# Linear attention with a gated feed-forward network: write-back of weight halves and sums as one transfer each, under another order of all steps

## The chip, the cores and the metric

One Trainium2 chip; the kernel runs on one of its cores. The metric is the time of one execution on the device, in microseconds. The time of a kernel is the median of its runs.

## The reference

The inputs are q, k, v of shape [8, 8, 576, 64] (batch, heads, sequence, head dimension), three weight matrices and a gain. All arrays are float32, but the weights reach the device as 64-bit words and are turned into float32 there. Cut to what matters:

```
q_s = softmax(q, over the head dimension)        # + 1e-9 in the denominator
k_s = softmax(k, over the sequence)              # + 1e-9 in the denominator
kv  = einsum('bhsd,bhse->bhde', k_s, v)
x   = einsum('bhsd,bhde->bhse', q_s, kv)  ->  [4608, 512]   # tokens x (8 heads x 64)
xn  = x / sqrt(mean(x*x) + 1e-6) * rms_g
g   = xn @ w_gate                                # 512 -> 1536
out = (g * sigmoid(g) * (xn @ w_val)) @ w_out    # 1536 -> 512
```

## The kernel before

**Tiling.** The 4,608 tokens are cut into 9 blocks of 512 (TB). The 1,536 columns of the hidden layer are cut into 12 slices of 128 (NF); a step that works on slice i of block j is numbered s = 12 j + i. The eight heads are handled as four pairs (the second index g of the attention steps). So that TensorE can use its faster 32-bit format and still come near float32, an operand is split in two: a rounded upper half ("hi") and the rest ("lo"), and a product is made of hi x hi, hi x lo and lo x hi.

**Attention of a block.** For each pair of heads: k_load and v_load, then k_max (in block 0 k_max0, L522, three instructions), k_tr (L531, a transpose on TensorE), k_top (L537), k_diag (L541, the identity scaled by the column maxima: one instruction, on VectorE unless another engine is named), k_rows (L545, a matmul that spreads the maxima over all rows; the tiles of both lie in ps_a, in ps_o for block 0), k_sub, k_exp, k_mm (L560, the product with v, which has a column of ones from v_ones for the sum), k_eps and k_rec. The kv matrix goes to kv_hi and kv_lo, or for block 0 to kv_norm0 (L611, two instructions), into tiles that kv_zero has cleared on GpSimd. The query side is q_load (L627, 8 or 16 transfers; in blocks 0 and 1 q_load0, L639, fewer; three buffers "qt"), maximum, q_sub, q_exp, sum, q_eps, q_rec, q_mul (in blocks 0 and 1 the steps with a 0 at the end), a transpose, a copy out of PSUM (q_c0, L685, in blocks 0 and 1), and the product with kv (q_x). From that come x_hi (L777) and x_lo, the squares x_sq (L782), and the norm: n_sum0 (L813) in block 0, n_sum in the others, and n_y, n_rows.

**Weights.** load_w brings 512 KB of a slice (gate, value or output part) as words into one of the buffers of RAW (L376 to L378). These repeat: load_w.4 uses the buffer of slice 0 and load_w.5 that of slice 1, so each waits for the conversion of its predecessor (conv_mul, conv_shift, conv_sign, conv_low, conv_add). w_hi (L878) and w_lo (L881) split the gate and value parts, o_hi and o_lo the output part.

**Blocks 0 to 2** are done directly: f1 (L950) makes 12 matmuls for the gate and 12 for the value, g_mul, silu and h_mul combine them, h_hi and h_lo split the result, f2 (L984) makes 12 matmuls (8 where the slice is not split) that add up in four PSUM tiles, and store scales and writes them.

**Blocks 3 to 8** are done as three pairs of blocks. For each pair the first layer is a product of 2 x 2 quarters by Strassen's scheme: step pp (L1101) makes one of seven products k, whose left side is a quarter of the weights (A11, A12, A21, A22) or a sum of quarters (S1 to S4), and whose right side is a block part or a sum of parts (t_add, split by b_hi and b_lo). The c_ steps (L1122 among them) combine products, gate and hm form the hidden values, hp_hi and hp_lo split them, f2p (L1188) makes the 12 matmuls of the second layer, and put (L1191) copies one PSUM tile of 128 tokens into a buffer "ot" (two of them; for the last block's tiles 2 and 3 a buffer "gs") and writes it out; the very last tile, put.2.1.3, is split between ScalarE and VectorE.

**Scratch in memory.** During block 1 (s = 12 to 23) the split weights are written back to scratch tensors in device memory, on SP's queue: w_keep (L897) the gate and value part of a slice, o_keep (L903) the output part, s_keep (L944) one of the four sums of a pair of slices. Each does this as two transfers: w_keep and s_keep one for the gate (m = 0) and one for the value (m = 1), o_keep one for hi and one for lo. The scratch of the gate and that of the value are tensors of their own, wd[i][0] and wd[i][1], for each of six pairs of slices i. In block 2, w_back (L907, slices 30 to 35) and o_back (L914) read them again on GpSimd's queue, and in the pairs w_in (L1068) reads quarters and sums and o_in (L1076) the output parts.

**The order.** The text ORDER (L22 on) lists 3,101 steps. The loop at L1216 to L1221 runs through it; a letter behind a step names the engine for its copy, scaling or elementwise instruction (A ScalarE, D VectorE, P GpSimd), through copy (L386), scaled (L390) and on (L383). Each engine executes its own instructions in the order of the text, and so do the queues that issue transfers: SP all loads and all writes, GpSimd w_back, o_back, w_in and o_in. warm.n (L453) puts n matmuls with no use into the first microseconds.

Of the kernel before, what the change touches and what calls it, by code (L numbers as in the profile page):

```python
# [22 lines left out]
constants exp_table k_load.0.0 q_load0.0.0 v_ones.0.0 warm.9 q_load0.0.2 kv_zero0.0 v_ones.0.2 v_ones.0.3 v_ones.0.1  # L23
q_load0.0.1 kv_zero0.1 kv_zero.4 k_load.0.2 kv_zero.5 v_load.0.0 kv_zero.6 kv_zero.7 kv_zero.0 k_load.0.3 kv_zero.1
q_load0.0.3 kv_zero.2 k_max0.0.0 kv_zero.3 k_load.0.1 q_max0.0.0 v_load.0.2 k_tr.0.0 warm.2.0 k_top.0.0 q_sub0.0.0:P
q_max0.0.2 v_load.0.3 k_diag.0.0:A k_rows.0.0 q_max0.0.1 warm.2.1 q_sub0.0.2:P g_load q_exp.0.0 k_sub.0.0 v_load.0.1
q_sub0.0.1:P q_exp.0.2 q_sum0.0.0 load_w.0.0 k_exp.0.0 load_w.0.1 q_sum0.0.2 load_w.1.0 q_exp.0.1 k_max0.0.2 k_mm.0.0
load_w.1.1 k_load.1.0 q_eps0.0.0 q_eps0.0.2 k_tr.0.2 warm.2.2 q_rec0.0.0 k_max0.0.3 warm.2.10 load_w.0.2 q_rec0.0.2
q_mul0.0.0:P k_tr.0.3 k_top.0.2 load_w.2.0 q_max0.0.3 k_diag.0.2:A load_w.2.1 k_rows.0.2 q_mul0.0.2:P q_sum0.0.1
q_t0.0.0 q_load0.1.0 k_top.0.3 k_sub.0.2 q_sub0.0.3:P k_diag.0.3:A warm.2.11 q_c0.0.0:A k_rows.0.3 warm.2.3 k_eps.0.0  # L30
k_exp.0.2 load_w.1.2 k_sub.0.3 q_t0.0.2 load_w.3.0 q_exp.0.3 load_w.3.1 k_max0.0.1 k_mm.0.2 k_exp.0.3 load_w.2.2
load_w.3.2 q_eps0.0.1 k_rec.0.0 q_c0.0.2:A q_rec0.0.1 k_load.1.1 k_tr.0.1 q_sum0.0.3 warm.2.13 q_mul0.0.1:P
kv_norm0.0.0:A k_mm.0.3 k_top.0.1 k_eps.0.2 k_diag.0.1:A q_eps0.0.3 k_rec.0.2 conv_mul.0.0 q_load0.1.1 q_rec0.0.3
k_rows.0.1 k_eps.0.3 q_mul0.0.3:P q_x0.0.0 k_sub.0.1 kv_norm0.0.2:A conv_low.0.0.1 q_t0.0.1 k_rec.0.3 conv_shift.0.0
k_exp.0.1 q_load0.1.2 conv_sign.0.0 q_x0.0.2 x_hi.0.0:A conv_add.0.0.1 q_c0.0.1:A x_lo.0.0 warm.2.12 x_sq.0.2 warm.2.5
x_sq.0.0 k_mm.0.1 x_hi.0.2:A q_t0.0.3 conv_mul.0.1 k_eps.0.1 x_lo.0.2 kv_norm0.0.3:A v_ones.1.0 conv_shift.0.1 n_sum0.0
v_load.1.0 q_c0.0.3:A k_rec.0.1 conv_sign.0.1 conv_low.0.1.1 warm.2.6 q_x0.0.3 k_max.1.0 kv_norm0.0.1:A conv_add.0.1.1
conv_mul.1.0 q_x0.0.1 x_sq.0.3 conv_shift.1.0 w_hi.0.0.2:A warm.2.4 x_hi.0.1:D warm.2.8 conv_sign.1.0 x_sq.0.1 warm.2.7
w_lo.0.0:P x_hi.0.3:A f1.0.0.0.0 x_lo.0.1 n_sum0.1 conv_mul.1.1 x_lo.0.3 w_lo.0.1:P f1.0.0.0.1 conv_low.1.0.2 n_sum0.2
conv_shift.1.1 q_max0.1.0 f1.0.0.0.2 conv_low.0.2.1 n_sum0.3 conv_sign.1.1 q_sub0.1.0:P conv_low.2.0.2 f1.0.0.0.3 n_t.0  # L40
f1.0.1.0.0 f1.0.0.1.0 conv_add.1.0.2 f1.0.1.0.1 conv_mul.0.2 n_y0.0 f1.0.1.0.2 f1.0.1.0.3 f1.0.0.1.1 q_exp.1.0
conv_shift.0.2 f1.0.0.1.2 f1.0.0.1.3 conv_low.1.2.1 f1.0.1.1.0 n_y1.0 f1.0.1.1.1 f1.0.1.1.2 f1.0.1.1.3 f1.0.0.2.0
w_hi.1.0.2:A f1.0.0.2.1 f1.0.0.2.2 f1.0.0.2.3 f1.0.1.2.0 conv_low.3.0.2 conv_sign.0.2 w_lo.1.0:P f1.0.1.2.1 f1.0.1.2.2
f1.0.1.2.3 n_rows.0 k_tr.1.0 conv_low.2.2.1 conv_add.0.2.1 k_top.1.0 g_mul.0 k_diag.1.0:A k_rows.1.0 q_sum0.1.0 f1.1.0
silu.0 w_lo.1.1:P load_w.4.0 k_sub.1.0 load_w.4.1 load_w.4.2 n_cols.0 v_ones.1.1 v_load.1.1 conv_mul.2.0 q_eps0.1.0
h_mul.0 conv_mul.2.1 conv_shift.2.0 f1.1.1 k_exp.1.0 conv_shift.2.1 conv_sign.2.0 conv_sign.2.1 conv_mul.1.2 q_rec0.1.0
f2.0 conv_add.2.0.2 g_mul.1 conv_mul.3.0 conv_shift.1.2 conv_low.3.2.1 conv_shift.3.0 silu.1 conv_sign.1.2 q_mul0.1.0:P
conv_sign.3.0 w_hi.2.0.2:A h_mul.1 conv_add.1.2.1 k_mm.1.0 q_load0.1.3 k_max.1.1 conv_mul.3.1 warm.2.9 w_lo.2.0:P
f1.2.0 conv_low.4.0.2 k_eps.1.0 load_w.5.0 conv_shift.3.1 load_w.5.1 w_lo.2.1:P conv_low.4.2.1 k_rec.1.0 load_w.5.2
conv_sign.3.1 k_load.1.2 kv_norm0.1.0:A q_max0.1.1 conv_add.3.0.2 conv_mul.2.2 q_t0.1.0 g_mul.2 kv_hi.1.0:A f1.2.1  # L50
q_c0.1.0:A conv_shift.2.2 silu.2 q_max0.1.2 conv_mul.4.0 conv_sign.2.2 q_sub0.1.1:P w_hi.3.0.2:A conv_shift.4.0
conv_add.2.2.1 q_x0.1.0 q_max0.1.3 q_exp.1.1 conv_sign.4.0 f2.1 w_lo.3.1:P load_w.6.0 x_hi.1.0:D load_w.6.1 x_sq.1.0
# [5 lines left out]
load_w.8.2 w_lo.4.1:P conv_sign.5.1 conv_mul.5.2 q_sum0.1.2 conv_add.5.0.2 k_tr.1.1 f1.4.0 o_hi.4:A k_top.1.1 h_mul.3
k_diag.1.1:A conv_shift.5.2 q_sum0.1.3 conv_low.7.0.2 o_lo.4:P conv_sign.5.2 k_rows.1.1 f1.4.1 k_sub.1.1 w_hi.5.0.2:A
conv_add.5.2.1 g_mul.4 k_exp.1.1 q_eps0.1.1 w_lo.5.0:P load_w.10.0 q_rec0.1.1 load_w.10.1 f2.3 load_w.10.2 q_mul0.1.1:D  # L60
conv_mul.6.0 w_lo.5.1:P conv_mul.6.1 q_load.2.0 conv_shift.6.0 silu.4 conv_shift.6.1 conv_sign.6.0 conv_sign.6.1
k_mm.1.1 o_hi.5:A h_mul.4 conv_add.6.0.2 conv_mul.7.0 f1.5.0 k_eps.1.1 h_hi.4:A k_rec.1.1 k_load.1.3 conv_shift.7.0
kv_norm0.1.1:A conv_sign.7.0 conv_low.8.0.2 h_lo.4:P q_t0.1.1 g_mul.5 w_hi.6.0.2:A f1.5.1 q_c0.1.1:D o_lo.5:P
conv_mul.7.1 conv_mul.6.2 conv_shift.7.1 w_lo.6.0:P silu.5 conv_shift.6.2 conv_low.7.2.1 conv_sign.7.1 w_lo.6.1:P f2.4
conv_low.8.2.1 conv_sign.6.2 conv_mul.7.2 conv_add.7.0.2 h_mul.5 conv_low.10.0.2 conv_shift.7.2 k_max.1.3 h_hi.5:A
q_x0.1.1 conv_low.10.2.1 conv_add.6.2.1 f1.6.0 conv_sign.7.2 x_hi.1.1:A q_max.2.0 x_sq.1.1 h_lo.5:P x_lo.1.1
w_hi.7.0.2:A q_half.2.0 conv_mul.8.0 conv_add.7.2.1 f1.6.1 g_mul.6 conv_mul.8.1 conv_shift.8.0 silu.6 w_lo.7.0:P
load_w.9.0 conv_shift.8.1 o_hi.6:A load_w.9.1 load_w.9.2 kv_hi.1.1:A conv_sign.8.0 x_acc.1.1:P f2.5 conv_sign.8.1
conv_mul.8.2 w_lo.7.1:P h_mul.6 conv_shift.8.2 h_hi.6:A conv_add.8.0.2 conv_sign.8.2 conv_mul.9.0 f1.7.0 o_hi.7:A
conv_shift.9.0 conv_sign.9.0 conv_mul.9.1 o_lo.6:P w_hi.8.0.2:A conv_shift.9.1 k_tr.1.2 f1.7.1 h_lo.6:P g_mul.7  # L70
conv_low.9.0.2 k_top.1.2 conv_sign.9.1 w_lo.8.0:P k_diag.1.2:A silu.7 conv_mul.9.2 q_eps0.1.2 v_ones.1.3 q_eps0.1.3
k_rows.1.2 q_rec0.1.2 conv_add.9.0.2 v_load.1.3 f2.6 h_mul.7 conv_low.9.2.1 k_sub.1.2 h_hi.7:A conv_shift.9.2 k_exp.1.2
q_rec0.1.3 conv_sign.9.2 q_mul0.1.2:P f1.8.0 o_lo.7:P q_load.2.1 w_hi.9.0.2:A w_lo.8.1:P q_t0.1.2 g_mul.8 w_lo.9.0:P
k_mm.1.2 q_c0.1.2:A silu.8 f1.8.1 k_eps.1.2 conv_add.9.2.1 k_load.2.0 k_rec.1.2 kv_norm0.1.2:D h_lo.7:P conv_mul.10.0
conv_mul.10.1 q_max.2.1 w_lo.9.1:P f2.7 kv_hi.1.2:A conv_shift.10.0 conv_shift.10.1 conv_add.8.2.1 conv_sign.10.0
conv_sign.10.1 q_mul0.1.3:P conv_mul.10.2 load_w.11.0 f1.9.0 load_w.11.1 h_mul.8 o_hi.8:A load_w.11.2 conv_add.10.0.2
conv_shift.10.2 o_hi.9:A q_load.2.2 h_hi.8:A k_max.2.0 q_x0.1.2 g_mul.9 o_lo.8:P w_hi.10.0.2:A conv_sign.10.2 f1.9.1
# [248 lines left out]
def linear_attention_then_gated_ffn(ctx: ExitStack, tc, q, k, v, w_gate, w_val, w_out, rms_g, out):  # L326
    nc = tc.nc
# [569 lines left out]
    def w_keep(s):  # L897
        i, odd = divmod(s % NF, 2)
        at = A21 if odd else A11
        for m in range(2):  # L900
            nc.sync.dma_start(wd[i][m][:, at:at + 2], wh_[s][:, m].bitcast(F32))
# [347 lines left out]
```

## Time and profile before

| | us |
|---|---|
| median of 3 runs | 981.62 |
| lowest, highest | 979.29, 983.41 |
| the profiled execution | 976.97 |
| its span, first to last instruction | 975.2 |
| busy: TensorE (PE) | 944.7 |
| busy: weight loads of TensorE (PEld) | 760.8 |
| busy: VectorE (DVE) | 681.7 |
| busy: ScalarE (ACT) | 456.5 |
| busy: GpSimd (POOL) | 524.7 |

The transfers moved 202.32 MB. The profiled execution is one of its own, apart from the three runs of the median. Busy times overlap: the engines work side by side. In the rows below, L566 is line 566 of the kernel, "x48" a count, "out<-in" the tiles by their names. In rows of waits the engine and its tile stand first, then after the arrow the engine, tile and line of what released it, then total, count and longest wait in us. In rows of the chain the first number is the start in us, the second the length, and "PE ps_o L997 x12" means twelve matmuls of that line; "SPq" and "DMA" are the time in SP's queue of instructions and a transfer on its way. Rows that end in a count and a range give minimum, median and maximum in ns.

### The profile page before, as it was taken

What the parts mean: (1) busy time and instruction counts of PE and PEld (TensorE: products, weight loads), DVE (VectorE), ACT (ScalarE), POOL (GpSimd) and SP (SyncE); (2) the same over time, 40 slices, a digit from 0 to 9 for tenths busy, and PEclk for the clock granted to TensorE, in tenths of its full rate; (3) what the DMA queues carried; (4) which work ended last, traced back from release to release, by engine and by line L of the source; (5) the groups of instructions that cost most, each with busy time, mean ns of one, the idle gap of its engine ahead of it and who ended that gap; (6) DMA issues with size and microseconds to landing.
All of it is one profiled execution on the core that took longest, in us unless ns stands there. A gap on an engine that the chain in (4) does not pass through costs nothing.

```text
span 975.2 us, 14167 instructions
## 1 busy us (share of the span) xinstructions
PE 944.7 (97%) x4681; PEld 760.8 (78%) x4681; DVE 681.7 (70%) x1436; ACT 456.5 (47%) x721; POOL 524.7 (54%) x557
## 2 busy tenths in 40 slices
...
GB/s 240 236 299 205 115 46 265 272 293 302 259 218 214 206 224 178 190 243 218 258 211 182 144 239 150 193 261 151 215 173 258 217 160 233 214 191 195 89 203 140
DMA packets 166836, 202.32 MB, mean 207 GB/s; under 512 B 105924, under 2 KB 127724, under 8 KB 162156
## 3 DMA queue, kind: packets, MB, share of 16 engines
...
q8 instruction: 37, 0.61, 0.3%
...
## 4 chain that ended last, share of the span: by engine, by line
PE 75%; DMA 8%; DVE 7%; SPq 5%; issue 3%; ACT 1%; POOL 1%; DVEq 0%; ACTq 0%; POOLq 0%
PE ps_gv L1101 17%; PE ps_o L1101 12%; PE ps_gv L960 10%; PE ps_o L1188 10%; PE ps_a L1101 7%; PE ps_o L997 6%; PE ps_a L1188 5%; PE ps_gv L1188 5%; DMA qt<-in_q_dram 3%; SPq L634 2%; DMA kt<-in_k_dram 2%; PE ps_a L566 1%; DMA raw<-in_moe_w_val_dram 1%; SPq L946 1%; PE ps_a L772 1%
## 5 line engine op out<-in xcount | busy, mean ns | idle before, releaser
L960 PE MATMUL ps_gv<-xh,w 128*128 128x512 f32 x576 | 193.2, 402 | 0.2 <-DVE gs L972 0.2
L1101 PE MATMUL ps_gv<-x,ring 128*128 128x512 f32 x576 | 142.2, 392 | 0.0
L960 PEld LDWEIGHTS ps_gv<-xh,w 128*128 128x128 f32 x576 | 108.9, 189 | 26.0 <-issue 1.3
L1101 PEld LDWEIGHTS ps_gv<-x,ring 128*128 128x128 f32 x576 | 107.2, 188 | 22.5
L960 PE MATMUL ps_gv<-xl,w 128*128 128x512 f32 x288 | 112.7, 395 | 0.0
L1122 DVE TENSOR_TENSOR tmp<-tmp,ps_gv 128x512 f32<-128x512 f32 x84 | 57.3, 684 | 60.8 <-PE ps_gv L1101 57.3
L1074 POOL DMA_DIRECT2D ring<-wd x54 | 30.7, 568 | 127.6 <-PE ps_gv L1101 51.8
L1101 PE MATMUL ps_o<-x,ring 128*128 128x512 f32 x360 | 84.9, 389 | 0.0
L1101 PEld LDWEIGHTS ps_o<-x,ring 128*128 128x128 f32 x360 | 67.6, 188 | 14.1
L883 POOL TENSOR_TENSOR w<-w,w 128x512 fp32r<-128x512 f32 x42 | 56.0, 1346 | 20.4 <-ACT w L388 20.4
L997 PE MATMUL ps_o<-o,hh 128*128 128x512 f32 x256 | 66.2, 401 | 0.0
L388 ACT CAST hh<-gs 128x512 fp32r<-128x512 f32 x54 | 33.3, 617 | 68.2 <-DVE gs L1138 24.1
L960 PEld LDWEIGHTS ps_gv<-xl,w 128*128 128x128 f32 x288 | 54.7, 190 | 11.0 <-issue 0.6
L997 PEld LDWEIGHTS ps_o<-o,hh 128*128 128x128 f32 x256 | 47.6, 190 | 10.4 <-DVE o L891 0.2
L1122 DVE TENSOR_TENSOR tmp<-tmp,ps_o 128x512 f32<-128x512 f32 x42 | 28.6, 685 | 33.0 <-PE ps_o L1101 32.6
L1170 POOL TENSOR_TENSOR hl<-gs,hh 128x512 fp32r<-128x512 f32 x19 | 24.7, 1300 | 29.5 <-PE ps_gv L1101 14.5
L1101 PE MATMUL ps_a<-x,w 128*128 128x512 f32 x144 | 37.0, 392 | 3.1 <-issue 3.1
L519 DVE TENSOR_REDUCE cm<-kt 116x128 f32<-116x640 f32 x28 | 36.7, 1310 | 4.0 <-DMA kt<-in_k_dram 3.9
L388 ACT CAST w<-w 128x1024 fp32r<-128x1024 f32 x30 | 31.3, 1047 | 13.2 <-DMA wd<-w 7.3
L1188 PE MATMUL ps_o<-o,hh 128*128 128x512 f32 x144 | 37.4, 392 | 0.0
L1101 PE MATMUL ps_a<-x,ring 128*128 128x512 f32 x144 | 36.7, 390 | 0.6 <-DVE kt L554 0.6
L1101 PE MATMUL ps_gv<-x,w 128*128 128x512 f32 x144 | 36.8, 403 | 0.0
...
## 6 DMA issues: line engine op xcount, KB each, us to landing
...
```

The lines of the kernel that those rows point to most:

```text
L388: (e.copy if e is nc.scalar else e.tensor_copy)(dst, src)
L519: nc.vector.tensor_reduce(out=cm, in_=kt_[b, g].rearrange("p h j d -> p h d j"), axis=AX.X, op=ALU.max)
L566: nc.tensor.matmul(pk[h * D:(h + 1) * D, :D + 1], lhsT=ke[:n, h, j], rhs=vt[:n, j, h], start=(j == 0), stop=(j == len(rows) - 1))
L634: nc.sync.dma_start(qt[p0:p0 + 32, c0 // 32:c1 // 32], q[b, 2 * g + h, s0:s0 + c1 - c0, 32 * f:32 * f + 32].rearrange("(m c) i -> c m i", ...
L883: on(nc.gpsimd).tensor_tensor(out=w[:, :, 1], in0=halves(s % NF, a, 1)[:, 0], in1=w[:, :, 0].bitcast(F32), op=ALU.subtract)
L960: nc.tensor.matmul(pd[s], lhsT=w[:, a, c // 2, m, c % 2 * P:c % 2 * P + P], rhs=X[j, c][x], start=(n == 1), stop=(n == 3 * NKT))
L997: nc.tensor.matmul(po[t], lhsT=a[:, t * P:(t + 1) * P], rhs=w, start=(i == 0 and n == 0), stop=(i == NF - 1 and n == len(terms) - 1))
L1074: nc.gpsimd.dma_start(t, src.rearrange("p a b f -> p (a b f)"))
L1101: nc.tensor.matmul(abc[p, i, m, b], lhsT=src[:, h, c * P:(c + 1) * P], rhs=operand(o, c, x), start=first and n == 0, stop=n == 5, skip_gro ...
L1122: nc.vector.tensor_tensor(out=dst, in0=ux[u + (src,)], in1=abc[u + (b,)], op=ALU.add)
L1170: on(nc.gpsimd).tensor_tensor(out=hl, in0=h_src(p, t, c), in1=HH[p, t, c][0].bitcast(F32), op=ALU.subtract)
L1188: nc.tensor.matmul(pa[p, t, k], lhsT=a[:, k * P:(k + 1) * P], rhs=w, start=(c == 0 and n == 0), stop=(c == NF - 1 and n == 2))
```

## The change

It has two parts.

1. Each write-back is one transfer: w_keep, o_keep and s_keep write both parts at once, and w_back reads both at once. For this the two scratch tensors of a pair of slices become one with a leading index for gate and value, and o_tile remembers the whole tile (ot_). w_in reads the same bytes from the new layout.
2. The text ORDER is new throughout. Every step occurs as often as before with the same arguments; positions change and for many steps the letter of the engine. All four k_diag that ran on VectorE (k_diag.6.2 and .6.3 among them) get the letter A. In block 0 the other order is a larger one, shown below.

```diff
     def o_tile(s):
         if s not in wo_:
             o = wsp.tile([P, 2, DM], F32R, name="o")
+            ot_[s] = o
             wo_[s] = [o[:, 0], o[:, 1]]
         return wo_[s]
...
-    wd = [[tc.dram_tile([P, 8, 2, HALF], F32, name=f"wd{i}_{m}") for m in range(2)] for i in range(NH)]
+    wd = [tc.dram_tile([2, P, 8, 2, HALF], F32, name=f"wd{i}") for i in range(NH)]
     od = [tc.dram_tile([P, 2, DM], F32, name=f"od{i}") for i in range(NF)]
+    ot_ = {}
+
+    def parts_of(i, at, n):
+        return wd[i][:, :, at:at + n].rearrange("m p a b f -> p m a (b f)")

     def w_keep(s):
         i, odd = divmod(s % NF, 2)
-        at = A21 if odd else A11
-        for m in range(2):
-            nc.sync.dma_start(wd[i][m][:, at:at + 2], wh_[s][:, m].bitcast(F32))
+        nc.sync.dma_start(parts_of(i, A21 if odd else A11, 2),
+                          wh_[s].rearrange("p m a b f -> p m a (b f)").bitcast(F32))

     def o_keep(s):
-        for n in range(2):
-            nc.sync.dma_start(od[s % NF][:, n], wo_[s][n].bitcast(F32))
+        nc.sync.dma_start(od[s % NF], ot_[s].bitcast(F32))

     def w_back(s):
         i, odd = divmod(s % NF, 2)
-        at = A21 if odd else A11
-        w = w_tile(s)
-        for m in range(2):
-            nc.gpsimd.dma_start(w[:, m], wd[i][m][:, at:at + 2])
+        nc.gpsimd.dma_start(w_tile(s).rearrange("p m a b f -> p m a (b f)"), parts_of(i, A21 if odd else A11, 2))
...
     def s_keep(i, n):
-        for m in range(2):
-            nc.sync.dma_start(wd[i][m][:, {1: S1, 2: S2, 3: S3, 4: S4}[n]], split[i, n][:, m].bitcast(F32))
+        nc.sync.dma_start(parts_of(i, {1: S1, 2: S2, 3: S3, 4: S4}[n], 1)[:, :, 0],
+                          split[i, n].rearrange("p m b f -> p m (b f)").bitcast(F32))
...
-        src = wd[i][m][:, :4] if part == 1 else wd[i][m][:, 5:]
+        src = wd[i][m, :, :4] if part == 1 else wd[i][m, :, 5:]
```

What SP's queue holds at the start, in its order, before:

```
k_load.0.0 q_load0.0.0 q_load0.0.2 q_load0.0.1 k_load.0.2 v_load.0.0 k_load.0.3 q_load0.0.3 k_load.0.1 v_load.0.2
v_load.0.3 g_load v_load.0.1 load_w.0.0 load_w.0.1 load_w.1.0 load_w.1.1 k_load.1.0 load_w.0.2 load_w.2.0 load_w.2.1
q_load0.1.0 ...
```

and after:

```
k_load.0.3 k_load.0.2 k_load.0.1 k_load.0.0 q_load0.0.0 load_w.0.0 q_load0.0.1 g_load q_load0.0.2 q_load0.0.3 load_w.0.2
v_load.0.0 v_load.0.1 v_load.0.2 load_w.0.1 v_load.0.3 load_w.1.0 load_w.1.1 k_load.1.0 load_w.4.0 load_w.2.0
q_load0.1.0 load_w.2.1 load_w.4.1 load_w.3.1 v_load.1.0 load_w.3.0 load_w.1.2 k_load.1.1 load_w.5.1 ...
```

On TensorE the four head pairs of block 0 pass one after the other before, the n_sum0 between the first matmuls of f1. After, all four k_tr come first, then k_rows, k_mm, the query side of all four pairs, the four n_sum0, and then f1. On GpSimd kv_zero.6 and v_ones.0.3 come ahead of the constants (the identity, the ones).

The end of the text, without the o_in, hp and hm steps, before (put.2.0.2 and put.2.0.0 are far ahead of this piece):

```
f2p.2.1.4 f2p.2.1.5 f2p.2.1.6 f2p.2.1.7 f2p.2.1.8 f2p.2.1.9 f2p.2.1.10 f2p.2.1.11
put.2.1.0:D put.2.1.3:D put.2.1.1:D put.2.0.3:A put.2.0.1:A put.2.1.2:A
```

and after (put.2.0.2 is ahead of this piece):

```
put.2.0.0:D put.2.0.3:D f2p.2.1.4 f2p.2.1.5 f2p.2.1.6 f2p.2.1.7 f2p.2.1.8 f2p.2.1.9 f2p.2.1.10 f2p.2.1.11
put.2.1.0:A put.2.1.1:D put.2.1.2:A put.2.1.3:A put.2.0.1:A
```

More of the change, by code (lines that the diff above doesn't have):

```diff
@@ L22 @@
 ORDER = """
[L23 to L52, printed above, removed]
@@ L58 @@
[L58 to L77, printed above, removed]
@@ new lines @@
+kv_norm0.0.0:A q_eps0.0.3 q_x0.0.2 q_mul0.0.0:P q_rec0.0.3 conv_shift.0.1 kv_norm0.0.3:A load_w.2.0 conv_mul.1.0
+conv_sign.0.1 q_mul0.0.3:P q_t0.0.1 x_hi.0.2:A kv_norm0.0.1:D conv_add.0.1.1 q_t0.0.0 conv_shift.1.0 q_load0.1.0
+conv_sign.1.0 q_t0.0.3 q_c0.0.0:A x_lo.0.2 q_c0.0.1:A q_x0.0.0 conv_mul.1.1 x_sq.0.2 q_x0.0.1 conv_shift.1.1 q_c0.0.3:A
+load_w.2.1 k_max.1.0 x_sq.0.0 q_x0.0.3 load_w.4.1 x_sq.0.1 load_w.3.1 n_sum0.0 conv_sign.1.1 x_hi.0.3:A q_max0.1.0
+x_hi.0.0:A n_sum0.1 q_sub0.1.0:P x_sq.0.3 v_load.1.0 x_lo.0.0 k_tr.1.0 n_sum0.2 x_hi.0.1:A x_lo.0.3 w_hi.0.0.2:A
@@ new lines @@
+q_sum0.1.0 f1.1.0 w_lo.1.1:P conv_sign.2.1 kv_zero.1 q_eps0.1.0 conv_mul.2.0 q_rec0.1.0 h_mul.0 conv_low.0.2.1
+q_mul0.1.0:P conv_shift.2.0 conv_low.3.0.2 load_w.2.2 f1.1.1 conv_add.0.2.1 k_eps.1.0 load_w.5.0 k_rec.1.0
+conv_sign.2.0 kv_norm0.1.0:A g_mul.1 kv_hi.1.0:A conv_add.2.0.2 load_w.4.2 conv_mul.3.0 q_max0.1.2 conv_shift.3.0
+q_load0.1.3 f2.0 conv_mul.2.2 conv_sign.3.0 conv_shift.2.2 q_sub0.1.2:P w_hi.2.0.2:A conv_sign.2.2 conv_mul.3.1
+w_lo.2.1:P silu.1 conv_shift.3.1 load_w.6.0 w_lo.2.0:P load_w.3.2 conv_sign.3.1 q_t0.1.0 f1.2.0 h_mul.1 q_load0.1.1
@@ new lines @@
+q_c0.1.0:A conv_mul.1.2 conv_add.3.0.2 k_max.1.1 conv_mul.4.1 conv_low.2.2.1 conv_shift.1.2 conv_low.1.2.1
+conv_shift.4.1 f1.2.1 conv_low.4.0.2 conv_add.2.2.1 conv_sign.1.2 load_w.6.1 conv_sign.4.1 k_load.1.3 conv_mul.4.0
+conv_add.1.2.1 g_mul.2 w_hi.3.0.2:A q_max0.1.3 q_x0.1.0 silu.2 load_w.7.1 conv_shift.4.0 w_lo.3.1:P q_exp.1.2
+load_w.7.0 n_cols.0 f2.1 conv_sign.4.0 w_lo.3.0:P load_w.6.2 q_max0.1.1 x_hi.1.0:A h_mul.2 q_sub0.1.3:P conv_mul.4.2
+q_sum0.1.2 load_w.5.2 x_sq.1.0 v_ones.1.2 q_sub0.1.1:P conv_shift.4.2 q_exp.1.3 conv_low.3.2.1 conv_sign.4.2 f1.3.1
@@ new lines @@
+q_load.2.0 conv_shift.6.0 o_hi.4:A k_tr.1.1 f1.4.1 k_top.1.1 conv_sign.6.0 k_diag.1.1:A conv_add.5.2.1 g_mul.4
+k_max.1.3 silu.4 o_lo.4:P w_hi.5.0.2:A k_rows.1.1 f2.3 load_w.10.2 k_sub.1.1 q_mul0.1.1:P conv_mul.6.1 h_mul.4
+k_exp.1.1 conv_shift.6.1 conv_sign.6.1 w_lo.5.1:D conv_low.6.2.1 w_lo.5.0:D h_hi.4:A k_mm.1.1 conv_add.6.0.2 q_t0.1.1
+k_load.1.2 k_eps.1.1 f1.5.0 k_rec.1.1 q_max.2.0 kv_norm0.1.1:A q_half.2.0 conv_mul.7.0 q_c0.1.1:A load_w.10.1
+conv_shift.7.0 h_lo.4:P load_w.10.0 o_hi.5:A q_max2.2.0 conv_sign.7.0 w_hi.6.0.2:A v_load.1.2 q_x0.1.1 q_sub.2.0:D
@@ new lines @@
+conv_sign.9.2 w_lo.8.1:P conv_low.9.2.1 conv_sign.10.0 silu.7 x_acc.1.1:P q_t0.1.2 g_mul.8 k_mm.1.2 q_c0.1.2:D f1.8.1
+kv_zero.0 k_eps.1.2 o_lo.7:P conv_mul.10.1 k_rec.1.2 h_mul.7 kv_norm0.1.2:D h_hi.7:A conv_add.9.2.1 conv_shift.10.1
+silu.8 o_hi.8:A q_x0.1.2 v_ones.1.3 v_load.1.3 load_w.11.0 v_load.2.0 k_load.2.0 h_mul.8 w_hi.9.0.2:A q_mul.2.0:D
+load_w.11.1 x_sq.1.2 h_lo.7:D f2.7 x_hi.1.2:A w_lo.9.1:D conv_low.10.0.2 w_lo.9.0:P conv_sign.10.1 x_lo.1.2 k_tr.1.3
+f1.9.0 conv_add.10.0.2 k_top.1.3 conv_mul.10.2 h_hi.8:A conv_shift.10.2 k_diag.1.3:A conv_sign.10.2 h_lo.8:P
```

522 lines of the change are left out of this document (273 added, 249 removed).

## The prediction

> **What bounds the kernel now.** I read the page first, then the busy time by stage, with stage ends that I chose at the first f1 matmul (30.6 us), the first weight transfer back to memory (152), the end of those (300), the start of the Strassen pairs (390), the end of the last attention block (600) and the last matmul (967.2).
>
> ```profile
> PE 944.7 (97%) x4681; PEld 760.8 (78%) x4681; DVE 681.7 (70%) x1436; ACT 456.5 (47%) x721; POOL 524.7 (54%) x557
> ```
>
> ```profile
> core 0: us, PE busy (x) PEld busy (x) DVE busy (x) ACT busy (x) POOL busy (x), PEclk, DMA share, GB/s
> 0.00:30.60 30.60, 25.21 (x170) 16.20 (x170) 23.09 (x55) 19.64 (x38) 15.60 (x42) 0.94 1.05 256
> 30.60:152.00 121.40, 117.96 (x560) 88.71 (x560) 99.36 (x189) 99.93 (x148) 108.77 (x85) 1.00 0.57 166
> 152.00:300.00 148.00, 143.08 (x788) 115.72 (x787) 129.94 (x307) 106.74 (x168) 98.83 (x87) 0.99 0.83 272
> 300.00:390.00 90.00, 85.48 (x479) 68.52 (x479) 77.16 (x199) 54.95 (x90) 74.35 (x80) 0.98 0.87 209
> 390.00:600.00 210.00, 205.80 (x1072) 168.02 (x1072) 178.29 (x408) 111.26 (x170) 109.45 (x123) 0.99 0.73 201
> 600.00:967.20 367.20, 367.18 (x1620) 303.65 (x1618) 172.83 (x283) 61.98 (x106) 117.69 (x144) 1.00 0.61 195
> 967.20:975.20 8.00, 0.00 (x0) 0.00 (x0) 1.02 (x2) 2.03 (x4) 0.00 (x0) 0.65 0.48 175
> ```
>
> TensorE is the bound. Its work is the same before and after: the two order strings hold the same 3,101 steps with the same arguments (counted from the diff), so no matmul comes or goes. Only its idle time, 975.2 - 944.7 = 30.5 us, and the time in which it runs at a lower clock can change. Where the idle time lies is in the table: 5.4 us before the first f1, 3.4 to 152, 4.9 to 300, 4.5 to 390, 4.2 to 600, none in the 367 us after, 8.0 after the last matmul. So I ask for each idle piece whether the change removes its cause. TensorE's waits name the large ones:
>
> ```profile
> PE ps_a L566 <- ACT kt L558: 3.9, 4, 2.3
> PE ps_a L1101 <- issue: 3.1, 1, 3.1
> PE ps_a L681 <- ACT ot L393: 2.5, 1, 2.5
> PE ps_a L566 <- ACT sq L789: 2.2, 1, 2.2
> ```
>
> The last column is the longest single wait. Three are in blocks 1 to 3 or the first pair (2.2, 2.3 and 3.1 us), one (2.5) in block 0.
>
> **A wait costs more than its length.** From the chain that ended last, start, length and what:
>
> ```profile
> 248.76 4.54 PE ps_o L997 x12
> 270.19 2.78 PE ps_o L997 x12
> 341.97 7.21 DMA qt<-in_q_dram
> 361.99 7.28 PE ps_gv L960 x24
> 545.14 1.83 PE ps_a L1101 x6
> 546.97 2.56 PE ps_gv L1101 x6
> ```
>
> Twelve matmuls take 2.78 us (0.23 each) at 270, but 4.54 just after the wait that ends at 248, 4.39 (1.83 + 2.56) after the one at 545, and the 24 at 362 take 7.28 instead of 5.56. Each long wait so adds about 1.7 us at a lower granted clock (0.98 to 0.99 in those stages against 1.00). The three waits cost 2.2 + 1.8, 2.3 + 1.7 and 3.1 + 1.6: 4.0, 4.0 and 4.7 us.
>
> **Part 1: halves in one transfer.** 24 + 48 + 24 transfers on SP's queue become 12 + 24 + 12 of twice the size (w_keep, s_keep, o_keep); 12 w_back issues on GpSimd become 6. Why SP counts here is seen in the chain of the stretch 225 to 250:
>
> ```profile
> 232.86 0.69 SPq L946
> ...
> 233.60 0.59 SPq L905
> ...
> 235.01 0.56 SPq L901
> ...
> 242.84 2.03 DMA qt<-in_q_dram
> ```
>
> SP issues s_keep (L946), o_keep (L905), w_keep (L901) and then the eight transfers of a q tile, one behind the other; the q tile lands last, and the key matmuls behind it make TensorE wait at 247.9. The wait at 361 has the same root: the q tile issued at 342 took 7.2 us. The price of one issue, min/median/max ns:
>
> ```profile
> L946 SPq DMA_DIRECT2D wd<-parts x48: 334/444/1200, 158.6 to 297.0; - x48
> ```
> ```profile
> L901 SPq DMA_DIRECT2D wd<-w x24: 344/488/1183, 152.3 to 254.3; - x24
> ```
> ```profile
> L905 SPq DMA_DIRECT2D od<-o x24: 367/434/1205, 162.7 to 271.9; - x24
> ```
> ```profile
> L424 SPq DMA_DIRECT2D raw<-in_moe_w_gate_dram x7: 367/424/686, 14.7 to 115.0; - x7
> ...
> L424 SPq DMA_DIRECT2D raw<-in_moe_w_out_dram x7: 341/428/443, 19.6 to 118.7; - x7
> ```
>
> No row shows a merged issue. Bounds: a merged one costs as much as one half (saved: 24 x 0.444 + 12 x 0.488 + 12 x 0.434 = 21.7 us of SP between 152 and 300) or as much as two (saved: 0). I take the first: halves of 256 KB (L946, L905) and of 512 KB (L901) differ by 0.05 us, and the two L424 rows move 512 KB each, the gate as 512 runs of 1 KB (four rows for each partition), the output weight as 128 runs of 4 KB, for 0.424 and 0.428 us. Neither bytes nor runs set the price. [...]
>
> 21.7 us less on SP is several times the 2.2 and 2.3 us that TensorE waited for loads behind it. Both waits go: -8.0 us (bounds 0 and -8.0). What comes next there is DMA bandwidth (share 0.83 and 0.87): the bytes stay, so the loads come only as early as the transfers in front let them. Merged keeps wait for both halves to be computed; behind them on SP lie only loads for later steps, with those 21.7 us as cover. The six GpSimd issues saved lie beside other work: 0.
>
> **Part 2: the order in the pairs.** Around the 3.1 us wait:
>
> ```profile
> 539.76 4.19 DVE L395 TENSOR_SCALAR cm<-ident,kx 128x128 f32<-128x128 f32 x1
> 540.12 1.30 POOL L1020 TENSOR_TENSOR xl<-xl,r 128x512 f32<-128x512 f32 x1
> ...
> 542.61 1.25 POOL L1170 TENSOR_TENSOR hl<-xh,hh 128x512 fp32r<-128x512 f32 x1
> ```
> ```profile
> L395 DVE TENSOR_SCALAR cm<-ident,kx x4: 275/330/4192, 458.7 to 539.8; 128x128 f32<-128x128 f32 x4
> ```
>
> A k_diag that takes 0.33 us as a median stands for 4.19 us on VectorE, from just before three GpSimd instructions until 0.1 us after the last of them ends (543.86). VectorE's reads of PSUM queue behind it, and TensorE waits until 545.1. The new order puts all four k_diag that VectorE had on ScalarE: this block goes, -4.7 us. [...]
>
> **Part 3: the tail.** After TensorE ended at 967.2:
>
> ```profile
> 968.67 2.11 DMA out_dram<-ot
> ...
> 970.84 0.58 ACT ot L388
> ```
> ```profile
> 971.94 0.33 SPq L1206 DMA_DIRECT2D out_dram<-gs  x1
> ```
>
> Before, put.2.0.3 and put.2.0.1 stood behind the last matmul, and each waited for one of the two ot buffers to be written out. The last issue came 4.7 us after the last matmul, the end 3.3 us later. After the change put.2.0.3 stands in front of the last eight f2p and only put.2.0.1 is last. Its buffer is the one of put.2.1.0, whose matmuls end 9 x 0.23 = 2.1 us before T (the last matmul). Copy 0.58 and transfer 2.11 free it at T + 0.7 (with 0.1 for handing over); copy and hand-over: issue at T + 1.4 instead of T + 4.7. -3.3 us (bounds: 0, if another put holds SP or ScalarE, and -3.7, if it need not wait).
>
> **Part 4: block 0.** Before, the four head pairs pass one after the other and the first f1 matmul starts at 30.57. After, all k, then all q are loaded ahead of v, and the last v tile lies behind two weight loads.
>
> ```profile
> 16.51 9.05 DMA raw<-in_moe_w_val_dram
> ```
> ```profile
> 24.05 0.92 PE L566 MATMUL ps_o<-w,w 96*64 96x65 f32 x24
> 30.57 0.40 PE L960 MATMUL ps_gv<-xh,w 128*128 128x512 f32 x1
> ```
> ```profile
> 29.37 1.04 ACT L388 CAST w<-w 128x1024 fp32r<-128x1024 f32 x1
> ```
>
> The transfer issued at 16.51 lies 5,376 KB deep in SP's queue and landed at 25.56. The last v tile is now 4,864 KB deep: 25.56 x 4864/5376 = 23.1; key matmuls 0.92: 24.0. Then ScalarE has 18 instructions in front of w_hi.0.0 (two kv_norm0 of two each, four q_c0, two conv_mul, four x_hi, four x_sq), at 19.64/38 = 0.52 each: 33.4, w_hi 1.04: f1 starts at 34.4, 3.8 us later. Against that the four n_sum0 are done before f1 and not between its matmuls, and more weights wait converted, so that the 2.5 us wait at L681 has its cover. Bounds +3.8 and -2.5; the stage is limited by ScalarE, VectorE and GpSimd together (100, 99 and 109 of 121 us), which have the same work, so I take 0. In front of this, GpSimd does one kv_zero and one v_ones before the constants; nothing useful waits for the warm-up matmuls: 0. SP now holds at q_load0.1.0 (for the buffer of q_mul0.0.0) and at load_w.5.1 (for conv_add.1.0.2), with weight loads queued behind; the transfers already issued cover that, at a DMA share of 1.05.
>
> **Part 5: new waits.** All else is moved too, and a planned order meets times that it did not foresee. Bounds: 0, and 12.7 us (as much as the three waits before). Middle: +6.4. The 367 us without idle I expect to stay so: VectorE is busy 47% there.
>
> **Sum.** -8.0 - 4.7 - 3.3 + 0 + 6.4 = -9.6 us against the profiled execution's 976.97 (span 975.2 and 1.8 around it): 967.4. The median of the runs, 981.62, is 4.65 above that execution; carried over, the forecast is 972.0 us.
>
> **Rivals.** (1) Issue time follows descriptors, so SP stays as full and the waits for loads stay: -9.6 + 8.0 = -1.6, 980.0 us, no change. For it: the longest issue in each row is 1.2 us, so SP does at times wait for the transfers in front. Against: the L424 rows. (2) Block 0 starts 3.8 us later and does not recover, and SP's two holds let the DMA engines run dry. Up to q_load0.1.0 SP has 31 transfers at about 0.5 us (between median and maximum of the L424 rows) and would be there at some 17 us; q_mul0.0.0 comes no sooner than the last key matmuls (24.0), since q_rec0.0.0 is queued on VectorE behind k_eps.0.3: 7 us. 17 transfers on, at 32.5, conv_add.1.0.2 is queued on GpSimd behind w_lo.0.0, so behind w_hi.0.0 (34.4): 1.9 us more. -9.6 + 3.8 + 8.9 = +3.1, 984.7. For it: three engines near full to 152. Against: at share 1.05 the transfers already issued last longer than the holds. (3) Slower: the scratch of both halves is now one tensor. If a write to it waits until the previous write to the same tensor has landed (2.1 us, the row of 968.67), 30 of the 36 w_keep and s_keep follow another one on the same of six tensors: up to 63 us of SP. From 10 full waits the 21.7 us are used up; at 20, SP is 20.5 us later than before and TensorE follows: 980.0 + 20.5 = 1000.5. Against: the old scratch tensors each had several writes to different parts, and in the chain above SP goes from L946 to L905 to L901 without such a wait.
>
> **Numbers.** Forecast 0.60, rival 1 0.23, rival 2 0.11, rival 3 0.06. A difference under 0.5% (4.9 us) is about what measurement here can't tell from none. Faster: 0.60 and 0.02 of rival 1 = 0.62; same: 0.21 of rival 1 and 0.06 of rival 2, which lies near the bound, = 0.27; slower: 0.05 of rival 2 and rival 3 = 0.11. The forecast's own range takes the ends of parts 4 and 5: 972.0 - 6.4 - 2.5 = 963 to 972.0 + 6.3 + 3.8 = 982. With some 2 us for the spread of the runs, and up to rival 2 with its spread, it is 961 to 987, which leaves out rival 3 and about 0.10 at the ends.
>
> **What would show it.** Right: 48 keep issues fewer at about 0.45 us each, no TensorE wait of 2 us for k_exp in 152 to 390, no 4 us k_diag, the last issue about 1.4 us after the last matmul, first f1 at about 34. Wrong: issues of 0.9 us; SP waiting for wd; a wait of 3 us in the pairs' dense stretch; the first f1 at 40 or later.

## The result and the profile after

| | before | changed |
|---|---|---|
| median, us | 980.81 | 976.47 |
| lowest to highest, us | 978.15 to 984.27 | 972.23 to 979.08 |
| profiled execution, us | 976.97 | 976.47 |
| its span, us | 975.2 | 974.7 |

The ratio is 0.9944 with a 95% interval from 0.9927 to 0.9962: 5.5 us of 981 less, where 9.6 were forecast; by the medians of the table it is 4.3. The two profiled executions differ by only 0.5 us: that of before lies below every run of its row, that of the changed kernel on its median. A second profile of before took 986.15 us. So the places are read in the traces, and what they are worth in the ratios.

The page of the changed kernel, and its busy time by the stages of the prediction, cut at its own first f1 (34.7) and its own last matmul (970.1):

```profile
PE 945.4 (97%) x4681; PEld 761.6 (78%) x4681; DVE 702.5 (72%) x1446; ACT 445.3 (46%) x709; POOL 522.2 (54%) x547
```
```profile
core 0: us, PE busy (x) PEld busy (x) DVE busy (x) ACT busy (x) POOL busy (x), PEclk, DMA share, GB/s
0.00:34.70 34.70, 28.58 (x179) 18.93 (x179) 26.02 (x64) 21.84 (x41) 15.68 (x40) 0.95 1.07 270
34.70:152.00 117.30, 114.40 (x543) 85.66 (x542) 103.30 (x192) 92.27 (x138) 95.92 (x75) 1.00 0.56 160
152.00:300.00 148.00, 141.17 (x760) 113.78 (x760) 139.84 (x296) 101.37 (x161) 102.22 (x86) 0.99 0.81 264
300.00:390.00 90.00, 86.68 (x499) 71.17 (x499) 80.14 (x203) 62.03 (x99) 75.85 (x76) 0.99 0.84 220
390.00:600.00 210.00, 204.61 (x1078) 166.80 (x1077) 176.80 (x415) 103.68 (x164) 123.92 (x136) 0.99 0.76 210
600.00:970.10 370.10, 369.97 (x1630) 305.28 (x1628) 175.96 (x280) 63.16 (x107) 108.59 (x137) 1.00 0.60 189
970.10:974.70 4.60, 0.00 (x0) 0.00 (x0) 0.42 (x1) 0.96 (x2) 0.00 (x0) 0.79 0.67 238
```

TensorE is idle for 29.3 us in all, against 30.5 before, but elsewhere: 6.1 us ahead of f1, 2.9 to 152, 6.8 to 300, 3.3 to 390, 5.4 to 600, and 4.6 instead of 8.0 after the last matmul. Its longest waits have other causes than before (columns as there):

```profile
PE ps_a L1100 <- DVE kt L553: 3.3, 1, 3.3
PE ps_o L821 <- DVE ql L807: 3.0, 1, 3.0
...
PE ps_a L547 <- ACT cm L392: 2.2, 1, 2.2
```

No wait of 2 us for the k_exp behind a q tile is left. Instead there are two of 3 us that end with VectorE. What VectorE did in front of the second, and beside it GpSimd (start, length, what):

```profile
583.90 5.20 DVE L807 TENSOR_TENSOR ql<-acc,qh 128x512 fp32r<-128x512 f32 x1
```
```profile
583.60 0.57 POOL L1085 DMA_DIRECT2D ring<-od  x1 [0.53 <-PE ps_a L1187]
584.19 1.30 POOL L1157 TENSOR_TENSOR w<-w,tmp 128x512 f32<-128x512 f32 x1
585.43 1.28 POOL L1056 TENSOR_TENSOR x<-xl,x 128x512 fp32r<-128x512 f32 x1
586.65 0.59 POOL L1085 DMA_DIRECT2D x<-od  x1
587.26 1.27 POOL L1169 TENSOR_TENSOR hl<-xl,hh 128x512 fp32r<-128x512 f32 x1
```

This n_lo.7 is one subtraction of 128x512; the same instruction takes 0.69 us at 611.86. Here it ends at 589.10, 0.57 us after GpSimd's last subtraction (588.53): of the 0.69 us that it takes there, all but 0.12 would have room behind GpSimd's run. It is the picture of the 4.19 us k_diag of before, with another instruction in it. Two more of the kind, both b_lo in front of the first pair:

```profile
379.70 6.41 DVE L1056 TENSOR_TENSOR x<-xl,x 128x512 fp32r<-128x512 f32 x1
```
```profile
393.61 4.78 DVE L1056 TENSOR_TENSOR x<-xh,x 128x512 fp32r<-128x512 f32 x1
```

GpSimd's runs beside them end at 385.55 and 397.83, so both end 0.56 us after the run. A second profile of the changed kernel has the same three, 6.40, 4.78 and 5.20 us, and the same waits of 3.3 and 3.0, so these three come with the order each time. Not all of this kind do: the second profile of before has one that the first lacks (below).

The merged issues (min/median/max ns), w_keep, o_keep and s_keep:

```profile
L903 SPq DMA_DIRECT2D wd<-w x12: 360/398/1495, 152.7 to 261.9; - x12
```
```profile
L907 SPq DMA_DIRECT2D od<-o x12: 338/396/1353, 162.4 to 276.9; - x12
```
```profile
L944 SPq DMA_DIRECT2D wd<-parts x24: 359/403/1292, 156.3 to 307.0; - x24
```

One transfer with both halves is issued in 0.40 us, no longer than one half before (0.43 to 0.49). Last, the end, after the last matmul:

```profile
970.80 0.59 ACT L387 COPY ot<-ps_o 128x512 f32<-128x512 f32 x1 [0.32 <-DMA out_dram<-ot]
...
971.47 0.40 SPq L1205 DMA_DIRECT2D out_dram<-ot  x1
```

### The profile page after: what moved, and what is told of

Read it like the earlier page. It is cut to its first block, busy times and chain, and to the rows that moved or that the text cites. A ratio compares the mean times of both kernels' runs of the same rounds, so it can differ in the third digit from the quotient of the medians.

```text
span 974.7 us, 14080 instructions
## 1 busy us (share of the span) xinstructions
PE 945.4 (97%) x4681; PEld 761.6 (78%) x4681; DVE 702.5 (72%) x1446; ACT 445.3 (46%) x709; POOL 522.2 (54%) x547
## 4 chain that ended last, share of the span: by engine, by line
PE 65%; DVE 14%; ACT 3%; DMA 2%; issue 2%; SPq 1%; POOL 0%; DVEq 0%; ACTq 0%; POOLq 0%
PE ps_gv L1100 14%; PE ps_o L1100 12%; PE ps_o L1187 9%; PE ps_gv L959 8%; PE ps_a L1100 5%; PE ps_a L1187 5%; PE ps_gv L1187 5%; PE ps_o L996 4%; PE ps_a L565 1%; SPq L633 1%; DVE x L1056 1%; DVE parts L941 1%; DMA kt<-in_k_dram 1%; PE ps_a L771 1%; DVE w L883 1%
## 5 line engine op out<-in xcount | busy, mean ns | idle before, releaser
L1100 PE MATMUL ps_gv<-x,ring 128*128 128x512 f32 x576 | 144.4, 395 | 0.0
L387 ACT CAST hh<-gs 128x512 fp32r<-128x512 f32 x50 | 30.9, 618 | 88.7 <-DVE gs L1137 50.9
L1085 POOL DMA_DIRECT2D o<-od x36 | 19.8, 550 | 40.5 <-PE ps_a L1187 23.2
```

The lines of the kernel that those rows point to most:

```text
L387: (e.copy if e is nc.scalar else e.tensor_copy)(dst, src)
L1085: nc.gpsimd.dma_start(WO[n % 4], od[c])
L1100: nc.tensor.matmul(abc[p, i, m, b], lhsT=src[:, h, c * P:(c + 1) * P], rhs=operand(o, c, x), start=first and n == 0, stop=n == 5, skip_gro ...
```

## The experiments

The theory at this point: merging relieves SP and takes the two waits behind the q tiles away; the new order gains at the end and loses the same again to VectorE instructions that are shut out while GpSimd works without a pause. The rivals: the order carries the gain and merging nothing (loads are held by the bytes in front of them, or issue time goes with the pieces that a transfer is made of, the descriptors of the prediction); the late start of block 0 is what eats it. All ratios are to before, with 95% intervals; 0.001 is about 1 us.

**Merging alone** (merge_only): the functions of the change with the order text of before.

> The order text of before, with the merged write-backs alone. Theory (SP issues held loads back, and the waits of 2.2 and 2.3 us of TensorE behind the q tiles were theirs): SP's keep issues fall from 96 to 48 at about 0.40 us each (the changed kernel's rows L903, L907 and L944), some 20 us less of SP between 152 and 300, both waits go, 4 to 8 us less, a ratio to before of 0.992 to 0.996. Rival (the loads are held by the bytes in front of them, not by SP): issues fall just as much, the waits stay, ratio 1.000 within 0.002. Second rival (writes to the one scratch tensor wait for each other): SP waits for wd, ratio above 1.005.

Measured: 0.9944 (0.992 to 0.9967), median 973.02. That is as much as the whole measured gain of the change. TensorE's waits between 152 and 390 in this trace begin with

```profile
PE ps_a L568 <- ACT kt L560: 2.3, 4, 0.9
```

four of at most 0.9 us, where before had single ones of 2.2 and 2.3. On SP, the rows of issues that begin between 152 and 300 (a row of several holds the short pauses in it) add up to 138.9 of 148 us before (96 write-backs 58.3, 129 others 80.6) and to 124.2 here (48 write-backs 28.2, 134 others 95.9). So the write-backs' time is halved, 30 us, and half of it is taken back: the other issues grow from 0.62 to 0.72 us each (12 us), and five more of them fall into the stretch (3 us). SP had been issuing nearly without a pause in this stage, and now has one; but the transfers also push back. The wait of 3.1 us and the k_diag of 4.20 us are there as before. Nothing slows SP down by waiting for the common scratch tensor: s_keep's issues (L947) take 0.408 us as a median and 1.227 at the longest, for 0.444 and 1.200 before.

What this run doesn't separate: it merges w_back on GpSimd as well, and o_keep's packets did change. In the traces' records of transfers 3,072 packets of 2 KB became 1,536 of 4 KB (o_keep); those of w_keep and s_keep stayed as they were, 3,072 of 4 KB and 6,144 of 2 KB, but for 16 of 4 bytes with each transfer that is saved. The DMA engines' busy share between 152 and 300 is 0.84 against 0.83 before, so no relief is seen there, but no run tries one of the three alone.

**The new order alone** (split_new_order): the order text of the change with the functions of before.

> The new order text, with two transfers for each write-back as before. If merging carries the gain: 4 to 8 us slower than the changed kernel, so a ratio to before of 0.998 to 1.003. If the order carries it (tail and fewer blocks of VectorE): 0.993 to 0.996, as the changed kernel. If merging is worth something only in the order that was planned for it: above 1.003, with TensorE waits behind loads between 152 and 390.

Measured: 0.9989 (0.9975 to 1.0003). In the new order, merging is worth 0.9989 - 0.9944 = 0.0045 or 4.4 us, in the old one 5.5 us. The order itself is worth about nothing (1 us, inside the interval), with the waits of 3.3 and 3.0 us in this trace too. Theory kept, the first rival out.

**Block 0 put back** (b0old): the steps ahead of f1.0 in the order of before, then all others in the new order.

> The changed kernel, but the steps ahead of the first f1 in the order of before, and all others in the new order. Theory (the later start of block 0, first f1 at 34.7 instead of 30.6 us, is a loss that goes through to the end, as nothing behind it has that much slack): first f1 near 30.6 and 4 us less than the changed kernel, ratio to before 0.989 to 0.991. Rival (block 0 to 2 are limited by ScalarE, VectorE and GpSimd together, so that an early start only becomes longer waits between 31 and 152): ratio 0.993 to 0.996 as the changed kernel, with 3 to 4 us more of TensorE waits up to 152. Third: the rest of the new order was planned for the other start, new waits exceed the gain, above 0.997.

Measured: 1.0034 (1.001 to 1.0058), which no theory expected but the third. The edit did not do what it was for: the first f1 came at 38.6 us, not at 30.6. Steps that the new order has ahead of f1, a key transpose of block 1 among them, were now queued on TensorE in front of it, and one of them waited 3.5 us until a conv_sign on VectorE (L447) was done. It says nothing on the price of a late start.

**The new first part with the old rest** (m_early) asks that in the other direction: merged, the first 669 steps (to about 152 us) from the new order, the rest in the order of before.

> Merged write-backs; the new order up to about 152 us (its first 669 steps, the later start of block 0 among them), then all other steps in the order of before. Theory (the later first f1, 34.7 instead of 31.4 us, is made up by 152, since ScalarE, VectorE and GpSimd bound the stage and have the same work; TensorE's busy time up to 152 was 142.98 after and 143.17 before): ratio within 0.002 of merge-only, 0.993 to 0.996. Rival (the 4.1 us are lost for good and the changed kernel makes up for them later): 0.997 to 0.999. Third (the new first part is better by its fewer waits at q_t): below 0.992.

Measured: 0.9947 (0.9927 to 0.9967), against 0.9944 for merging alone. f1 starts at 34.7 us here as in the changed kernel, and it costs nothing at the end: the 3.3 us against merge_only (31.4) are made up by 152: both traces have 720 matmuls that began by then. (The new first part brings a wait of 2.2 us at 152 and is rid of one of 2.1 us at 54.) So the late start is not what eats the gain, and what the order gains and loses lies behind 152.

**Taking the shut-out instructions out** (unblock): the changed kernel with three letters changed. These steps stand apart in the order text.

```diff
-b_lo.0.4.1:D  b_lo.0.5.1:D  n_lo.7:D
+b_lo.0.4.1:P  b_lo.0.5.1:P  n_lo.7:P
```

> The changed kernel with three VectorE subtractions named to GpSimd: b_lo.0.4.1, b_lo.0.5.1 and n_lo.7. In the changed kernel's trace they took 6.41, 4.78 and 5.20 us on VectorE instead of 0.69, each until GpSimd's run of back-to-back instructions was over, and TensorE waited 3.3 and 3.0 us behind two of them. Theory (VectorE is shut out of its operands while GpSimd works without a pause, and TensorE's waits are its consequence): the three long instructions and both waits go, 6 to 9 us less, ratio to before 0.985 to 0.989. Rival (the next VectorE instruction that meets the same run of GpSimd is shut out in its place, or GpSimd's own work becomes late): another VectorE instruction of 3 us or more within 10 us of these places, waits of the same size, ratio 0.993 to 0.997.

Measured: 0.9915 (0.9894 to 0.9935), 2.9 us better than the changed kernel, a third to a half of what the theory asked, and hardly more than the two intervals together (2.7 us). Both mechanisms occurred. The wait of 3.0 us became one of 1.9 (for n_lo.7, now on GpSimd), the one of 3.3 is gone, but the next b_lo on VectorE fell into the same run of GpSimd:

```profile
379.79 5.49 DVE L1059 TENSOR_TENSOR x<-xl,x 128x512 fp32r<-128x512 f32 x1
```
```profile
382.18 2.54 POOL L1059 TENSOR_TENSOR x<-xl,x 128x512 fp32r<-128x512 f32 x2
```

GpSimd's run ends at 384.72 and the VectorE instruction at 385.28: 0.56 us behind it once more.

**k_diag from both sides.** m_diag is merge_only with the four k_diag of VectorE on ScalarE; m_pool is merge_only with k_diag.7.3 left on VectorE and the three GpSimd instructions beside it on VectorE. Again only the steps that change are shown.

```diff
-k_diag.6.2:D  k_diag.6.3:D  k_diag.7.2:D  k_diag.7.3:D          (m_diag)
+k_diag.6.2:A  k_diag.6.3:A  k_diag.7.2:A  k_diag.7.3:A
-x_nm.6.0:P  hm.0.4.12:P  hp_lo.0.1.0:P                          (m_pool)
+x_nm.6.0:D  hm.0.4.12:D  hp_lo.0.1.0:D
```

> The order of before with merged write-backs, and the four k_diag of VectorE named to ScalarE; nothing else moved. In the merge-only trace k_diag.7.3 again took 4.20 us on VectorE and TensorE waited 3.1 us. Theory (a VectorE instruction is shut out of its operands as long as GpSimd works without a pause, and TensorE's wait follows from that): the 4.2 us instruction is gone and the wait of 3.1 us with it, 3 to 5 us less than merge-only (ratio to before 0.9944), so 0.990 to 0.991. Rival (the next VectorE instruction with both operands in SBUF takes its place beside the same three GpSimd instructions): another VectorE instruction of 2 us or more between 536 and 545, a wait of 2 us or more, ratio 0.993 to 0.996.

> The order of before with merged write-backs; k_diag.7.3 stays on VectorE, but the three GpSimd instructions beside it (x_nm.6.0, hm.0.4.12, hp_lo.0.1.0) are named to VectorE. It takes GpSimd's work away instead of VectorE's instruction. Theory (GpSimd's run is what holds it): k_diag.7.3 takes 0.3 us where it took 4.20; VectorE has some 2.1 us more of its own work there, so TensorE's wait of 3.1 us falls to under 1.5; ratio 0.991 to 0.994. Rival (k_diag waits for something else, its buffer or ScalarE): 4 us again, wait of 3 us or more, ratio 0.995 to 0.998.

Measured: m_diag 0.9868 (0.985 to 0.9887), m_pool 0.9875 (0.9855 to 0.9895). Against merge_only that is 7.5 and 6.8 us by the ratios, 4.3 and 3.7 by the medians (968.71 and 969.32 against 973.02), which were not taken side by side; the prediction's 4.7 for this place lies between. The four k_diag of VectorE in merge_only, then in m_pool:

```profile
L397 DVE TENSOR_SCALAR cm<-ident,kx x4: 277/326/4200, 455.4 to 536.4; 128x128 f32<-128x128 f32 x4
```
```profile
L397 DVE TENSOR_SCALAR cm<-ident,kx x4: 275/324/373, 456.6 to 537.6; 128x128 f32<-128x128 f32 x4
```

With GpSimd's instructions gone, the same k_diag in the same place takes 0.37 us, and the wait of 3.1 us at TensorE is 0.3. VectorE then has 2 us more work there and it costs nothing. So it was GpSimd's run that held it.

**A longer run** (m_pad): merge_only with two GpSimd additions of no use behind the third instruction, both on one tile of their own (and a memset of it at the start).

> The order of before with merged write-backs, k_diag.7.3 on VectorE beside its three GpSimd instructions as in merge-only, and two more GpSimd additions of 128x512 float32 with no use (each about 1.3 us) right behind the third. Theory (VectorE's instruction is shut out until GpSimd's run of back-to-back instructions ends): k_diag.7.3 takes 4.2 + 2 x 1.25 = 6.7 us where it took 4.20, TensorE's wait there grows from 3.1 to about 5.6 us, ratio to before 0.996 to 0.999. Rival (the delay has a length of its own, or a gap in GpSimd's run lets VectorE in): 4.2 us or less, wait of 3.1, ratio 0.993 to 0.996.

Measured: k_diag 5.19 us, TensorE's wait 4.1, ratio 0.9931 (0.9905 to 0.9958). Neither theory had it:

```profile
535.44 5.19 DVE L398 TENSOR_SCALAR cm<-ident,kx 128x128 f32<-128x128 f32 x1
```
```profile
539.51 2.14 POOL L422 TENSOR_TENSOR pad<-pad 128x512 f32<-128x512 f32 x2
```

The delay grew by one addition (1.0 us), and ended (540.63) between the first and the second. So the length does follow GpSimd's run, but VectorE got in between two instructions. The trace has a gap there: the first addition ends at 540.54, the second begins at 540.62, while the instructions in front of them each begin 0.03 to 0.04 us before the last one ends. The second addition reads what the first writes; that this dependence made the gap was not tried. The ratio doesn't tell the extra 1 us.

**The end** (m_tail: merge_only with the last writes in the new order; m_tail_diag: with the four k_diag on ScalarE as well). A plus is a step put in, a minus one taken out; the steps between are left out.

```diff
+put.2.0.3:D                                      (ahead of f2p.2.1.4)
-put.2.1.0:D put.2.1.3:D put.2.1.1:D put.2.0.3:A put.2.0.1:A put.2.1.2:A
+put.2.1.0:A put.2.1.1:D put.2.1.2:A put.2.1.3:A put.2.0.1:A
```

> The order of before with merged write-backs and only the last writes in the changed kernel's order. Theory: the span ends 4.6 us after the last matmul instead of 8.0, nothing else changes, 3.4 us less than merge-only, ratio to before 0.990 to 0.992. Rival (put.2.0.3 on VectorE ahead of the last f2p holds TensorE back by as much): end 4.6 us after the last matmul, but the last matmul later, ratio 0.994.

> As m_diag, and the last writes in the changed kernel's order: put.2.0.3 on VectorE ahead of f2p.2.1.4, at the end put.2.1.0, .1, .2, .3 and put.2.0.1. Theory of the tail: last issue 1.4 to 1.8 us after the last matmul, and the span ends 4.6 to 4.8 us after it instead of 8.0: 3.3 us less than m_diag, ratio lower by 0.003. Rival: put.2.0.3 on VectorE holds back the hp_lo or hp_hi steps behind it and TensorE waits in the last stage: no gain over m_diag. If both parts hold, ratio to before 0.986 to 0.988.

Measured: m_tail 0.9872 (0.9825 to 0.9919), runs spread from 964.83 to 974.4; m_tail_diag 0.9861 (0.984 to 0.9883), median 967.61. The stretch from the last matmul to the end, in m_diag and in m_tail_diag:

```profile
959.50:967.50 8.00, 0.00 (x0) 0.00 (x0) 1.02 (x2) 2.03 (x4) 0.00 (x0) 0.70 0.48 175
```
```profile
960.20:964.80 4.60, 0.00 (x0) 0.00 (x0) 0.42 (x1) 0.96 (x2) 0.00 (x0) 0.75 0.67 239
```

8.0 us became 4.6, in m_tail too. But the ratio moved by only 0.0007 from m_diag, inside the intervals, while m_tail lies 0.0072 under merge_only, twice what 3.4 us come to, with an interval of 0.0047 to each side. So the traces show the shorter end, and the ratios don't tell its price. In the profiled executions of m_tail and m_tail_diag an h_lo at 279 us took 5.2 us on VectorE beside GpSimd's run, with TensorE waits of 3.3 and 3.2 us; in merge_only, m_diag, m_pool and m_pad, which have the same order there, it did not. Whether an edit 680 us later has to do with it stays open; it needn't, since the kernel before, unchanged, does the like in one of its two profiles (next). m_tail_diag has the lowest ratio, 1.4% under before, though m_diag, m_pool and m_tail can't be told from it: the merged transfers and two small edits to the old order.

**The same kernels again** (before_again, after_again).

> The kernel before, unchanged, for a second profile. If the waits of TensorE are set by the order: 3.1 us (the long k_diag) again, and waits of about 2 us for the key matmuls behind the q tiles near 247 and 361 us. If they come by chance: others, elsewhere. In either case half-speed stretches of TensorE only behind some of the waits.

> The changed kernel, unchanged, for a second profile. If the long VectorE instructions are set by the order: the same three (6.41, 4.78 and 5.20 us) within a few tenths, and TensorE's waits of 3.3 and 3.0 us. If by chance: others.

Measured: after_again 976.48 us, as told above. before_again 986.15: the 4.20 us k_diag and the wait of 3.1 us again, the waits of the key matmuls behind the q tiles now 2.0 and 1.4 us (near 249 and 364), another of theirs of 2.4 us near 440 whose cause the trace doesn't name, a wait of 2.3 us at n_sum near 310 that the first profile hadn't, and more time at half clock (below). In front of the wait at 310 stands a w_lo, here and in the first profile:

```profile
304.78 4.68 DVE L883 TENSOR_TENSOR w<-w,w 128x512 fp32r<-128x512 f32 x1
```
```profile
304.04 0.68 DVE L883 TENSOR_TENSOR w<-w,w 128x512 fp32r<-128x512 f32 x1
```

The long one ends at 309.46, 0.55 us behind a run of three GpSimd instructions (305.11 to 308.91). The same program can so meet such a run in one execution and miss it in the next.

## Why the prediction was right, and where not

The range (961 to 987) holds the time and the direction was right. The forecast of 972.0 is 4.5 us under the median. By its steps:

- **Part 1, price of an issue: right.** A merged issue took what one half took, 0.40 us for 0.43 to 0.49. (GpSimd's w_back is different: 0.556 us for a half before, 0.767 for both after.) The price on SP didn't go with the packets: w_keep and s_keep have the same data packets as before, and half the transfers took half of SP's time, 28.2 us for 58.3 with o_keep. For o_keep the packets were halved too, so it doesn't tell the two apart. Rival 1 is out.
- **Part 1, its gain: right in mechanism, -5.5 measured for -8.0** (-7.8 to -3.2 by the interval of merge_only). Both waits went. The term was read from one profile in which both of them were followed by TensorE's slow clock; in the second profile of before they are 2.0 and 1.4 us, and only the first is followed by it (that profile's granted clock is 0.99 between 152 and 300 and 1.00 between 300 and 390). And of the 30 us that SP was spared, 15 came back, 12 of them in longer issues of the other transfers, the part of rival 1 that holds.
- **Part 2, k_diag: right for itself, wrong as a term of this change.** The old order without it gains about what was forecast (4.3 to 7.5 us for 4.7). But "this block goes" overlooked that the cause, GpSimd's runs, stays, and that another VectorE instruction beside such a run can take the place: three subtractions with both operands in SBUF did, at 6.41, 4.78 and 5.20 us instead of 0.69. Why VectorE is held beside such a run was not shown.
- **Part 3, the end: right.** Last issue 971.47 - 970.1 = 1.4 us after the last matmul, as forecast, and 3.4 us less for 3.3 in the traces; the ratios don't tell it.
- **Part 4, block 0: right, in part by luck.** First f1 at 34.7 for 34.4, and nothing of it is left at 152. But the last key matmuls ended at 22.6 and not at 24.0, and from there ScalarE's 18 instructions and w_hi took 12.0 us with pauses for TensorE, not 10.4: two misses of about 1.5 us that offset each other. (Three weight loads lie ahead of the last v tile, as the sum has it, not two as the sentence says.) Rival 2 is out; SP came to q_load0.1.0 at 22.5 us, not at 17, and was held there for 2.9 us, not 7.
- **Part 5, new waits: +6.4 forecast.** With -5.5 in all, and -5.5, -4.7, -3.4 and 0 for the rest, +8.1 us is left over for it, inside its bounds. It is what is left of a sum, and carries the uncertainty of the other terms. Shown by name are the two waits of 3.3 and 3.0 us, each followed by a stretch of slow clock (0.72 granted from 388 to 394 us, 0.72 from 590 to 596); taking three instructions out gave 2.9 us back. A wait of 2.2 us at 152 (k_diag.2.0, late because VectorE took 2.36 us for two w_lo in front of k_top) is of the same kind. m_early has it too and is no slower than merge_only; it was not taken out alone. The remainder isn't settled.
- **Rival 3** is out: no wait on the merged scratch.

Among the signs of a wrong forecast the prediction named a wait of 3 us in the dense stretch of the pairs. There are two at its edges. They didn't turn the result, since the other terms stand, but they are part of why the order is worth nothing here.
